# The end of an attention and two-layer mixture kernel: products in TensorE's gaps, another order of the merge, four banks for the last results

## The chip, the cores and the metric

The kernel runs on one core of a Trainium2 chip. A core has TensorE for matrix products (weights are loaded by its own instruction, which the profile shows as PEld), VectorE (DVE), ScalarE (ACT), GpSimd (POOL) and SyncE (SP), which here only starts transfers. Products end in PSUM, which has eight banks; VectorE and ScalarE read them from there. The metric is the device time of one launch, in microseconds (us), the median of several runs.

## The reference

Three layers follow one another. The first is windowed attention over 4 sequences of 576 tokens with 8 heads of 64. Its output is a table of 2304 tokens by 512. The second layer is gated: `sigmoid(x @ w_gate) * (x @ w_val) @ w_out` with an inner width of 1536. The third is a soft mixture of 8 experts with 4 slots each:

```python
logits = x @ phi                                  # 2304 x 32 slots
d = logits - logits.max(0, keepdims=True)         # softmax over the tokens, per slot
d = np.exp(d)
d /= d.sum(0, keepdims=True) + 1e-09
slot_input = (d.T @ x).reshape(E, S_per_e, D)     # 32 slots x 512
for e in range(E):
    h = np.maximum(slot_input[e] @ w1[e], 0.0)    # 4 x 1024
    slot_out[e] = h @ w2[e]                       # 4 x 512
c = logits - logits.max(1, keepdims=True)         # softmax over the slots, per token
c = np.exp(c)
c /= c.sum(1, keepdims=True) + 1e-09
return c @ slot_out                               # 2304 x 512
```

The softmax over the tokens runs over all 2304 tokens, so the expert products can start only when the last token block has been seen.

## The kernel before

The tokens are worked in five blocks: four of 512 and a short one of 256 (the last 64 tokens of each sequence). Attention, the gated layer (`l1`, `l2`) and the slot sums (`moe2`) go through the blocks, interleaved in the order of the program. A scheduler may move an instruction forward on its engine when its inputs and buffers allow; `tc.keep_in_program_order` takes that freedom from an instruction. Each engine then works its list strictly in order, TensorE too.

`moe2(n, last)` (L456) takes a block's second-layer output. It transposes it (tp), forms the logits (lt_ps), and keeps a running maximum mrun, sum lrun and slot sum acc per slot, in the manner of an online softmax: nm holds the new maximum and the factor that scales what was there; d is the exponential of the logits less the maximum, dt its transpose, and sp the block's share of the slot sum. Tokens are held in up to four groups of 32 rows, one for each 128 tokens, with maxima of their own. For the last block `merge` (L432) brings the four groups together: it transposes mrun (rows), takes the maximum over the groups, subtracts, takes the exponential (L448), and turns the four weights back into a column (wcol) and a 128 x 32 table i4w. With it, st_ps (L660) sums acc over the groups, and the result, st, is what the experts read.

The expert layer follows. h_ps (L670) is the product with w1 for all 8 experts, with four column groups at a time; after it come ht_ps, so_ps (L729, with w2, first for the left 256 columns of the output, dh = 0, then for the right, dh = 1), `scale` (by the reciprocal of the sums), `gather` (sr_ps: the sum over column groups, split into two parts), and `result` (L751): the product op of each token's weights ct with sr, for two token tiles at a time into one of the two PSUM banks of the pool ps_l1. ScalarE copies the first two tiles of a block to ob, VectorE the other two, and SP sends ob to memory: 512 KB for each of the four large blocks, and four transfers of 64 KB for the short one. The left half's results are put between the so_ps products of the right half. The weights of the experts come in 32 transfers of 1 MB as buffers come free (`load_e`).

At the very start of the kernel `keep_warm` (L110) lets TensorE multiply a table of zeros in bfloat16 while it waits for its first data.

## Time and profile before

| | us |
|---|---|
| median of 3 runs | 621.69 (621.18 to 622.74) |
| the profiled execution, its own time | 622.22 |
| its span, first to last instruction | 620.4 |
| TensorE busy (share of the span) | 593.7 (96%) |
| VectorE busy | 305.5 (49%) |
| ScalarE busy | 269.2 (43%) |
| GpSimd busy | 185.6 (30%) |

The span is what the trace covers; the time of the launch is 1.82 us longer. Busy shares are means over the whole span. The last 68 us, from the end of the second layer for the short block, are the stretch in which the change lies. The granted clock over the whole span is 0.977 of full speed. In a timeline's row the bracket at the end says how long the engine was idle before it and which instruction ended that; a row may join several instructions (x48).

### The profile page before, as it was taken

What the parts mean: (1) busy time and instruction counts of PE and PEld (TensorE: products, weight loads), DVE (VectorE), ACT (ScalarE), POOL (GpSimd) and SP (SyncE); (2) the same over time, 40 slices, a digit from 0 to 9 for tenths busy, and PEclk for the clock granted to TensorE, in tenths of its full rate; (3) what the DMA queues carried; (4) which work ended last, traced back from release to release, by engine and by line L of the source; (5) the groups of instructions that cost most, each with busy time, mean ns of one, the idle gap of its engine ahead of it and who ended that gap; (6) DMA issues with size and microseconds to landing.
All of it is one profiled execution on the core that took longest, in us unless ns stands there. A gap on an engine that the chain in (4) does not pass through costs nothing.

```text
span 620.4 us, 11601 instructions
## 1 busy us (share of the span) xinstructions
PE 593.7 (96%) x4849; PEld 454.5 (73%) x4849; DVE 305.5 (49%) x544; ACT 269.2 (43%) x456; POOL 185.6 (30%) x147
## 2 busy tenths in 40 slices
PE   7898999999999999999999999999999899988994
PEld 4667777777777776777788888888878789863452
DVE  5978565645344556574422232312455666662342
ACT  3798454353535454555322122312454485540122
POOL 1344435432134542461101010302534524431100
PEclk9899999999999999999999999999999999996996
DMA  8988759882244351669010011028313724787965
GB/s 348 375 312 277 257 171 396 300 310 67 69 179 163 123 187 46 226 214 364 17 69 28 41 68 69 0 78 327 138 69 148 280 81 173 299 342 300 423 236 199
DMA packets 24933, 120.46 MB, mean 194 GB/s; under 512 B 2480, under 2 KB 7344, under 8 KB 14768
## 3 DMA queue, kind: packets, MB, share of 16 engines
q1 hardware_dynamic: 24880, 119.71, 52.2%
q8 instruction: 38, 0.62, 0.4%
q14 instruction: 15, 0.12, 0.1%
HBM read 105.55 MB, written 14.16 MB: 193 GB/s over the span
## 4 chain that ended last, share of the span: by engine, by line
PE 79%; ACT 6%; POOL 5%; issue 5%; DVE 3%; DMA 2%; ACTq 0%; DVEq 0%; POOLq 0%; SPq 0%
PE l1ps L372 46%; PE acc L411 13%; POOL l2t L404 4%; PE xp L192 3%; PE h_ps L670 3%; PE so_ps L729 2%; PE s_ps L139 2%; ACT l2t L402 2%; PE tr L177 1%; PE tp L467 1%; ACT bd L180 1%; PE op L760 1%; PE lt_ps L475 1%; PE sp L513 1%; DMA qk<-qkv 1%
## 5 line engine op out<-in xcount | busy, mean ns | idle before, releaser
L372 PE MATMUL l1ps<-x_hi,whl 128*128 128x512 f32 x768 | 248.6, 397 | 0.0
L372 PEld LDWEIGHTS l1ps<-x_hi,whl 128*128 128x128 f32 x768 | 144.8, 189 | 31.7 <-issue 0.4
L411 PE MATMUL acc<-l2t 128*128 128x512 f32 x648 | 159.4, 397 | 1.6 <-POOL l2t L404 1.6
L372 PE MATMUL l1ps<-x_lo,whl 128*128 128x512 f32 x384 | 150.7, 392 | 0.0
L411 PEld LDWEIGHTS acc<-l2t 128*128 128x128 f32 x648 | 118.6, 188 | 27.8 <-POOL l2t L404 2.0
L404 POOL TENSOR_TENSOR l2t<-wos,l2t 128x512 fp32r<-128x512 f32 x54 | 72.1, 1338 | 124.3 <-ACT l2t L402 120.7
L384 DVE TENSOR_TENSOR g<-l1ps,g 128x512 f32<-128x512 f32 (+1 forms) x60 | 38.2, 637 | 135.0 <-PE l1ps L372 134.9
L407 DVE TENSOR_TENSOR l2t<-g,l2t 128x512 fp32r<-128x512 f32 (+1 forms) x60 | 66.0, 1100 | 53.5 <-ACT l2t L406 52.6
L372 PEld LDWEIGHTS l1ps<-x_lo,whl 128*128 128x128 f32 x384 | 72.6, 189 | 14.2
L382 ACT ACTIVATE g<-l1ps 128x512 f32<-128x512 f32 (+1 forms) x60 | 33.3, 555 | 105.7 <-PE l1ps L372 105.5
L339 POOL TENSOR_TENSOR whl<-wst,whl 128x512 fp32r<-128x512 f32 x28 | 38.4, 1372 | 131.0 <-ACT whl L338 131.0
L402 ACT CAST l2t<-wos 128x512 fp32r<-128x512 f32 x60 | 37.0, 620 | 80.2 <-PE acc L411 27.0
L326 POOL TENSOR_TENSOR fw<-fw 128x512 int32<-128x512 int32 x36 | 49.1, 1373 | 75.7 <-DVE fw L324 33.6
L338 ACT CAST whl<-wst 128x512 fp32r<-128x512 f32 x56 | 31.9, 618 | 36.5 <-PE l1ps L372 28.0
L339 DVE TENSOR_TENSOR whl<-wst,whl 128x512 fp32r<-128x512 f32 x28 | 36.4, 1302 | 14.5 <-ACT whl L338 14.5
L372 PE MATMUL l1ps<-x,whl 128*128 128x256 f32 x288 | 36.4, 286 | 0.8 <-ACT g L382 0.5
L372 PEld LDWEIGHTS l1ps<-x,whl 128*128 128x128 f32 x288 | 35.1, 192 | 1.5 <-ACT g L382 0.7
L406 ACT CAST l2t<-g 128x512 fp32r<-128x512 f32 (+1 forms) x60 | 34.4, 573 | 1.7 <-DVE g L384 1.6
L192 PEld LDWEIGHTS xp<-bd,v 128*64 128x64 f32 x608 | 20.2, 139 | 13.6 <-ACT bd L180 9.0
L192 PE MATMUL xp<-bd,v 128*64 128x64 f32 (+1 forms) x608 | 23.6, 228 | 5.4 <-ACT bd L180 3.6
L180 ACT COPY bd<-tr 64x512 f32<-64x512 f32 x40 | 23.1, 578 | 8.0 <-PE tr L177 7.7
L152 DVE TENSOR_REDUCE mx<-s_ps 128x4 f32<-128x256 f32 x40 | 15.5, 418 | 21.7 <-PE s_ps L139 21.7
(128 smaller groups left out, 505.2 us busy)
## 6 DMA issues: line engine op xcount, KB each, us to landing
ew<-w SPq DMA_DIRECT2D x32, 1024.0 KB, 7.0
st<-wd SPq DMA_DIRECT2D x18, 1024.0 KB, 7.6
wos<-wo SPq DMA_DIRECT2D x15, 1024.0 KB, 4.7
wst<-wg SPq DMA_DIRECT2D x14, 1024.0 KB, 4.8
v<-qkv SPq DMA_DIRECT2D x20, 512.0 KB, 7.4
wg<-fw SPq DMA_DIRECT2D x12, 512.0 KB, 8.2
qk<-qkv SPq DMA_DIRECT2D x10, 576.0 KB, 4.9
qk<-qkv SPq DMA_DIRECT2D x8, 528.0 KB, 3.7
```

The costliest lines, as they stand in the source:

```text
L192: nc.tensor.matmul(o, lhsT=v[:, t, i, r, :], rhs=b_[:, 2 * r + t, i, :, 0:nq], start=True, stop=True)
L326: nc.gpsimd.tensor_tensor(low.bitcast(I32), top.bitcast(I32), low.bitcast(I32), ALU.add)
L338: nc.scalar.copy(whl[:, 0, h], src[:, h])
L339: (nc.gpsimd if pool[h] else nc.vector).tensor_tensor(whl[:, 1, h], src[:, h], whl[:, 0, h].bitcast(F32), ALU.subtract)
L372: nc.tensor.matmul(pt[:, 0:nt], lhsT=whl[:, w_, a, dc, :], rhs=x_[n][:, dc, :], start=first, stop=(dc == HP_ORDER[-1] and w_ == 1),)
L382: nc.scalar.activation(g, pt[:, 0:nt], AF.Sigmoid)
L384: nc.vector.tensor_tensor(g, pt[:, 0:nt], g, ALU.mult)
L402: nc.scalar.copy(woh, wos[:, f % 4])
L404: eng.tensor_tensor(wol, wos[:, f % 4], woh.bitcast(F32), ALU.subtract)
L406: nc.scalar.copy(gh[:, 0:nt], g)
L407: nc.vector.tensor_tensor(gl[:, 0:nt], g, gh[:, 0:nt].bitcast(F32), ALU.subtract)
L411: nc.tensor.matmul(accs[j], lhsT=g_[:, c], rhs=w_, start=(f == 0 and g_ is gh and w_ is woh), stop=(f == NF - 1 and g_ is gl),)
```

## The change

- `keep_busy(count)` issues bfloat16 products of 512 columns on TensorE, from the mask table that lies in SBUF from the start, into a bank that nobody reads: 2 behind the last block's transposes, 4 behind its logits, 2 behind wcol, 2 behind st_ps, and 4 behind the last sr_ps. 14 in all.
- `merge` is split. In the last block d, its exponential and its transpose come first, then the merge's maximum, subtraction and exponential (`merge_rows`), and wcol and i4w (`merge_weights`) come behind sp. The update of acc is done in two halves of 256 columns in the last block. In the other blocks the transpose of d also comes ahead of its sum.
- `result` takes PSUM banks from ps_a as well as from ps_l1: for the left half the short block's, for the right half every second pair of pairs, so that four banks take turns. The left half's short block comes behind the last so_ps products.
- The right half's four transfers of the short block are issued by ScalarE, not by SP.
- Some instructions are kept in program order.

TensorE's list from the logits of the last block to the expert layer, before (x_5128 is the last block's second-layer output, t_5161 the tile that holds the merge's pieces and st):

```order
L475 MATMUL lt_ps<-xt,cst 32x128 x8
L438 MATMUL rows<-cst,mrun 1x128
L450 MATMUL wcol<-cst,t_5161 128x1
L508 MATMUL dt_ps<-cst,d 128x64
L513 MATMUL sp<-x_5128,dt 32x512 x2
L660 MATMUL st_ps<-t_5161,acc 128x32 x4
L691 MATMUL sums<-cst,lrun 1x128
L670 MATMUL h_ps_5202<-ew,t_5161 32x512 x4
```

The same stretch of TensorE's list now, from the last of the four products behind the logits to st_ps:

```order
L124 MATMUL busy<-msk 128x512
L516 MATMUL dt_ps<-cst,d 128x64
L451 MATMUL rows<-cst,mrun 1x128
L530 MATMUL sp<-x_5128,dt 32x512 x2
L466 MATMUL wcol<-cst,t_5175 128x1
L124 LDWEIGHTS msk
L124 MATMUL busy<-msk 128x512
L124 LDWEIGHTS msk
L124 MATMUL busy<-msk 128x512
L681 MATMUL st_ps<-t_5175,acc 128x32 x4
```

dt_ps stands ahead of rows and wcol, wcol stands behind sp, and two added products stand between wcol and st_ps.

ScalarE's list in the same stretch, before (nm is the running maximum's factor, t_5161 here the merge's exponential):

```order
L493 ACT_TABLE_LOAD
L493 ACTIVATE nm<-nm 64x1
L448 ACTIVATE t_5161<-t_5161 1x128
L499 ACTIVATE d<-d 64x128
L535 ACTIVATE c<-c 128x64
```

And now:

```order
L510 ACT_TABLE_LOAD
L510 ACTIVATE nm<-nm 64x1
L514 ACTIVATE d<-d 64x128
L461 ACTIVATE t_5175<-t_5175 1x128
L556 ACTIVATE c<-c 128x64
```

The exponentials of d and of the merge have changed places.

TensorE's list at the end of the right half, before (ct_5267 holds the short block's token weights):

```order
L729 MATMUL so_ps_5336<-ew,ht 32x256 x8
L760 MATMUL op<-sr,cts 128x256 x4
L760 MATMUL op<-sr,ct_5267 128x256 x2
L729 MATMUL so_ps_5336<-ew,ht 32x256 x16
L745 MATMUL sr_ps<-t_5161,cst 128x256
L760 MATMUL op<-sr,cts 128x256 x16
```

And now, up to the first of the four products behind sr_ps:

```order
L751 MATMUL so_ps_5348<-ew,ht 32x256 x8
L790 MATMUL op<-sr,cts 128x256 x4
L751 MATMUL so_ps_5348<-ew,ht 32x256 x16
L790 MATMUL op<-sr,ct_5279 128x256 x2
L769 MATMUL sr_ps<-t_5175,cst 128x256
L124 LDWEIGHTS msk
L124 MATMUL busy<-msk 128x512
```

The left half's short block has gone from ahead of the last 16 so_ps products to behind them.

```diff
--- before.py
+++ after.py
@@ -112,6 +112,19 @@
             nc.tensor.matmul(idle, lhsT=zero[:, 0:P], rhs=zero[:, 512:1024], start=True, stop=True)
 
     keep_warm(WARM)
+    busy = {}
+
+    kept = tc.keep_in_program_order
+
+    def keep_busy(count):
+        if "ps" not in busy:
+            busy["ps"] = ps_a.tile([P, 512], F32, tag="a", name="busy")
+        for _ in range(count):
+            kept(
+                nc.tensor.matmul(
+                    busy["ps"], lhsT=msk[:, M_ID:M_COLS], rhs=msk[:, 0:512], start=True, stop=True, skip_group_check=True
+                )
+            )
 
 
     x_hi, x_lo = {}, {}
@@ -429,7 +442,7 @@
     share = []
     first_pb = [True]
 
-    def merge():
+    def merge_rows():
         t1 = b8("l2", [P, 2048], F32, "t1")
         st, so = t1[:, 0:1152].rearrange("p (k x) -> p k x", k=ND), t1[:, 1152:1664]
         sc_ = t1[:, 1664:2048]
@@ -437,7 +450,7 @@
         rows = ps_m.tile([1, P], F32, tag="m", name="rows")
         nc.tensor.transpose(rows, mrun, ident)
         rm = sc_[0:1, 0:32]
-        nc.vector.tensor_reduce(rm, rows.rearrange("o (j s) -> o s j", j=4), AX.X, ALU.max)
+        kept(nc.vector.tensor_reduce(rm, rows.rearrange("o (j s) -> o s j", j=4), AX.X, ALU.max))
         re = sc_[0:1, 32:160].rearrange("o (j s) -> o j s", j=4)
         nc.vector.tensor_tensor(
             re,
@@ -446,12 +459,12 @@
             ALU.subtract,
         )
         nc.scalar.activation(re, re, AF.Exp)
+        return st, so, sc_, re, sc_[:, 160:192]
+
+    def merge_weights(re, i4w):
         wcol = ps_m.tile([P, 1], F32, tag="m", name="wcol")
         nc.tensor.matmul(wcol, lhsT=re.rearrange("o j s -> o (j s)"), rhs=ident[0:1, 0:1], start=True, stop=True)
-        i4w = sc_[:, 160:192]
         nc.vector.tensor_tensor(i4w, i4, wcol.to_broadcast([P, 32]), ALU.mult)
-        return st, so, sc_, re, i4w
-
 
     def moe2(n, last):
         xs = x2_sb.pop(n)
@@ -469,6 +482,8 @@
                 nc.vector.tensor_copy(xt[:, j], tp)
             else:
                 nc.scalar.copy(xt[:, j], tp)
+        if last:
+            keep_busy(2)
         lt_ps = ps_m.tile([P, P], F32, tag="m", name="lt_ps")
         for kc in range(ND):
             for j in range(ntt):
@@ -481,6 +496,8 @@
                 )
         lt = cpool.tile([P, P], F32, tag="lt", name="lt", bufs=2)
         nc.vector.tensor_copy(lt[0:np_], lt_ps[0:np_])
+        if last:
+            keep_busy(4)
         first = first_pb[0]
         first_pb[0] = False
         nm = sm.tile([P, 4], F32, tag="nm", name="nm")
@@ -492,11 +509,15 @@
             nc.vector.tensor_tensor(nm[0:np_, 1:2], mrun[0:np_], nm[0:np_, 0:1], ALU.subtract)
             nc.scalar.activation(nm[0:np_, 1:2], nm[0:np_, 1:2], AF.Exp)
             nc.vector.tensor_copy(mrun[0:np_], nm[0:np_, 0:1])
-        if last:
-            merged = merge()
         d = cpool.tile([P, P], F32, tag="d", name="d")
         nc.vector.tensor_scalar(d[0:np_], lt[0:np_], mrun[0:np_, 0:1], None, ALU.subtract)
         nc.scalar.activation(d[0:np_], d[0:np_], AF.Exp)
+        dt_ps = ps_m.tile([P, P], F32, tag="m", name="dt_ps")
+        nc.tensor.transpose(dt_ps[:, 0:np_], d[0:np_], ident[0:np_, 0:np_])
+        dt = cpool.tile([P, P], F32, tag="dt", name="dt")
+        nc.vector.tensor_copy(dt[:, 0:np_], dt_ps[:, 0:np_])
+        if last:
+            merged = merge_rows()
         if first:
             nc.vector.tensor_reduce(lrun, d, AX.X, ALU.add)
         else:
@@ -504,10 +525,6 @@
             nc.vector.scalar_tensor_tensor(
                 lrun[0:np_], lrun[0:np_], nm[0:np_, 1:2], nm[0:np_, 2:3], ALU.mult, ALU.add
             )
-        dt_ps = ps_m.tile([P, P], F32, tag="m", name="dt_ps")
-        nc.tensor.transpose(dt_ps[:, 0:np_], d[0:np_], ident[0:np_, 0:np_])
-        dt = cpool.tile([P, P], F32, tag="dt", name="dt")
-        nc.vector.tensor_copy(dt[:, 0:np_], dt_ps[:, 0:np_])
         sp = ps_m.tile([P, 512], F32, tag="m", name="sp")
         for j in range(ntt):
             nc.tensor.matmul(
@@ -516,9 +533,13 @@
         if first:
             nc.vector.tensor_copy(acc, sp)
         else:
-            nc.vector.scalar_tensor_tensor(
-                acc[0:np_], acc[0:np_], nm[0:np_, 1:2], sp[0:np_], ALU.mult, ALU.add
-            )
+            if last:
+                merge_weights(merged[3], merged[4])
+                keep_busy(2)
+            for c in (slice(0, 256), slice(256, 512)) if last else (slice(0, 512),):
+                nc.vector.scalar_tensor_tensor(
+                    acc[0:np_, c], acc[0:np_, c], nm[0:np_, 1:2], sp[0:np_, c], ALU.mult, ALU.add
+                )
         if last:
             return merged, lt
         shares(n, ntt, lt)
@@ -662,6 +683,7 @@
         st.rearrange("p k (e x) -> p k e x", x=36)[:, :, :, 0:4],
         st_ps.rearrange("p k (e a) -> p k e a", a=4),
     )
+    keep_busy(2)
     h_ps = [ps_a.tile([P, 512], F32, tag="a", name=f"h_ps{h}") for h in range(2)]
     reuse = ["qk", "qk", "v", "v", "xb", "xb", "ga", "gb", "gb", "gb"]
     for e in range(8):
@@ -726,13 +748,15 @@
     def expert(dh, e):
         for fc in range(8):
             c = fc % 4
-            nc.tensor.matmul(
+            ins = nc.tensor.matmul(
                 so_ps[dh][32 * c : 32 * c + 32],
                 lhsT=ht[fc // 4][:, c, 32 * e : 32 * e + 32],
                 rhs=ew[1, dh, e].rearrange("p a c -> p (a c)")[:, 256 * fc : 256 * fc + 256],
                 start=(e == 0 and fc < 4),
                 stop=(e == 7 and fc >= 4),
             )
+            if dh:
+                kept(ins)
 
     def scale(dh):
         so_, _ = half(dh)
@@ -742,22 +766,28 @@
     def gather(dh):
         so_, sr_ = half(dh)
         sr_ps = ps_m.tile([P, 256], F32, tag="m", name="sr_ps")
-        nc.tensor.matmul(sr_ps, lhsT=ones32, rhs=so_, start=True, stop=True)
+        kept(nc.tensor.matmul(sr_ps, lhsT=ones32, rhs=so_, start=True, stop=True))
         nc.scalar.copy(sr_, sr_ps)
         nc.vector.tensor_tensor(sr_[64:P], sr_ps[64:P], sr_[64:P].bitcast(F32), ALU.subtract)
 
     obs = {}
+    n_op = [0]
+    Z_ORDER = (0, 1, 2, 3, 4)
 
     def result(dh, z):
         _, sr_ = half(dh)
         n, ntt, ct = ct_sb[z]
-        if z % 2 == 0:
-            obs[dh] = b8(("x2", "ws", "ws")[z // 2], [P, 2, 4, 256], F32, "ob")
-        ob = obs[dh][:, z % 2]
+        k = Z_ORDER.index(z)
+        if k % 2 == 0:
+            obs[dh] = b8(("x2", "ws", "ws")[k // 2], [P, 2, 4, 256], F32, "ob")
+        ob = obs[dh][:, k % 2]
         for j in range(0, ntt, 2):
-            op = ps_l1.tile([P, 2, 256], F32, tag="l1", name="op")
+            more = k == 4 if dh == 0 else n_op[0] // 2 % 2
+            n_op[0] += dh
+            pool, tag = (ps_a, "a") if more else (ps_l1, "l1")
+            op = pool.tile([P, 2, 256], F32, tag=tag, name="op")
             for y in range(2):
-                nc.tensor.matmul(op[:, y], lhsT=ct[:, j + y], rhs=sr_, start=True, stop=True)
+                kept(nc.tensor.matmul(op[:, y], lhsT=ct[:, j + y], rhs=sr_, start=True, stop=True))
             if j == 0:
                 nc.scalar.copy(ob[:, j : j + 2], op)
             else:
@@ -767,7 +797,7 @@
             nc.sync.dma_start(out[576 * n : 576 * n + 512, d].rearrange("(a p) d -> p a d", p=P), ob)
         else:
             for b in range(4):
-                nc.sync.dma_start(
+                (nc.scalar if dh else nc.sync).dma_start(
                     out[576 * b + 512 : 576 * b + 576, d], ob[64 * (b % 2) : 64 * (b % 2) + 64, b // 2]
                 )
 
@@ -782,11 +812,14 @@
         expert(1, e)
         if e == GA:
             gather(0)
-        if GA < e <= GA + 5:
-            result(0, e - GA - 1)
+        if GA < e <= GA + 4:
+            result(0, Z_ORDER[e - GA - 1])
+    result(0, Z_ORDER[4])
     scale(1)
     gather(1)
-    for z in range(5):
+    busy["ps"] = ps_m.tile([P, 512], F32, tag="m", name="busy")
+    keep_busy(4)
+    for z in Z_ORDER:
         result(1, z)
 
 
```

## Rows read from the trace of the kernel before

**Rows 1.** Timeline of TensorE, last block to expert layer; columns: start, length (us), engine, line, ...
```profile
554.94 1.39 PE L475 MATMUL lt_ps<-xt,cst 128*32 128x128 f32 x16 [0.35 <-DVE xt L469]
557.66 0.27 PE L438 MATMUL rows<-cst,mrun 128*1 128x128 f32 x1 [1.33 <-DVE mrun L494]
558.95 0.58 PE L450 MATMUL wcol<-cst,t 1*128 1x1 f32 x2 [1.02 <-ACT t L448]
559.47 0.37 PE L508 MATMUL dt_ps<-cst,d 64*128 64x64 f32 x1
560.15 1.92 PE L513 MATMUL sp<-x,dt 128*32 128x512 f32 x4 [0.32 <-DVE dt L510]
562.91 1.92 PE L660 MATMUL st_ps<-t,acc 128*128 128x32 f32 x8 [0.84 <-DVE acc L519]
564.64 0.40 PE L691 MATMUL sums<-cst,lrun 128*1 128x128 f32 x1
565.28 6.78 PE L670 MATMUL h_ps<-ew,t 128*32 128x512 f32 x48 [0.24 <-DVE t L661]
...
576.08 5.36 PE L670 MATMUL h_ps<-ew,t 128*32 128x512 f32 x48
```

**Rows 2.** Stretches: PE, PEld, DVE, ACT, POOL busy (count); granted clock; DMA share; GB/s.
```profile
556.00:558.00 2.00, 0.59 (x6) 0.14 (x2) 1.32 (x7) 0.72 (x2) 0.00 (x0) 0.99 0.97 410
558.00:560.00 2.00, 0.88 (x3) 0.68 (x3) 0.95 (x5) 0.51 (x2) 0.00 (x0) 0.50 1.05 442
...
566.00:568.00 2.00, 2.00 (x16) 0.55 (x12) 0.56 (x3) 0.00 (x0) 0.00 (x0) 0.50 0.04 8
568.00:570.00 2.00, 2.00 (x24) 0.52 (x20) 0.00 (x0) 0.00 (x0) 0.00 (x0) 0.95 0.86 246
```

**Rows 3.** Timeline of TensorE, the last result.
```profile
603.47 0.51 PE L760 MATMUL op<-sr,ct 128*128 128x256 f32 x2 [0.44 <-ACT ob L762]
603.90 1.93 PE L729 MATMUL so_ps<-ew,ht 128*32 128x256 f32 x32
606.71 0.70 PE L745 MATMUL sr_ps<-t,cst 128*128 128x256 f32 x2 [0.87 <-ACT t L740]
608.33 0.73 PE L760 MATMUL op<-sr,cts 128*128 128x256 f32 x4 [0.93 <-DVE sr L747]
609.55 1.22 PE L760 MATMUL op<-sr,cts 128*128 128x256 f32 x4 [0.49 <-ACT ob L762]
```

**Rows 4.** Stretches of half a microsecond at the end, same columns as rows 2.
```profile
610.50:611.00 0.50, 0.28 (x2) 0.00 (x0) 0.18 (x1) 0.47 (x1) 0.00 (x0) 0.50 0.39 141
611.00:611.50 0.50, 0.47 (x2) 0.48 (x2) 0.50 (x1) 0.00 (x0) 0.00 (x0) 0.50 1.09 389
...
618.50:619.00 0.50, 0.00 (x0) 0.00 (x0) 0.00 (x0) 0.00 (x0) 0.00 (x0) 0.50 0.51 131
```

**Rows 5.** Timeline of VectorE, then of ScalarE: copies of the last result.
```profile
609.10 0.69 DVE L764 COPY ob<-op 128x512 f32<-128x512 f32 x1 [0.82 <-PE op L760]
...
614.89 0.59 ACT L762 COPY ob<-op 128x512 f32<-128x512 f32 x1 [0.93 <-PE op L760]
```

**Rows 6.** Timeline of SP's queue: the short block's transfers, first and second half.
```profile
604.62 3.22 SPq L770 DMA_DIRECT2D out<-ob  x4
...
615.50 2.40 SPq L770 DMA_DIRECT2D out<-ob  x4
```

**Rows 7.** Timeline of VectorE, then of ScalarE, beside rows 1.
```profile
557.55 0.28 DVE L498 TENSOR_SCALAR d<-lt,mrun 64x128 f32<-64x128 f32 x1
...
562.12 0.74 DVE L519 SCALAR_TENSOR_TENSOR acc<-acc,nm,sp 64x512 f32<-64x512 f32 x1 [1.91 <-PE sp L513]
...
558.59 0.31 ACT L448 ACTIVATE t<-t 1x128 f32<-1x128 f32 x1 [1.02 <-DVE t L442]
558.81 0.29 ACT L499 ACTIVATE d<-d 64x128 f32<-64x128 f32 x1
```

**Rows 8.** Timeline of TensorE near the start: bfloat16 products of 512 columns.
```profile
8.49 0.81 PE L112 MATMUL idle<-zero 128*128 128x512 bf16 x3
```

## The prediction

> **What bounds the kernel now.** I read the page first, then TensorE's order of time for the last 70 us, then the same stretch on VectorE and ScalarE, then the granted clock in short stretches, and last the output queue. The page says that TensorE is busy for 593.7 of 620.4 us, so most of the kernel is its work, and the change does not touch that work. What it touches is the end, where TensorE waits in two places.
>
> The first place lies between the last output product of the last token block and the first product of the expert layer, h_ps, at 565.28. There TensorE runs short products, each of which waits for another engine [rows 1]: 1.33 us before rows, 1.02 us before wcol (released by ScalarE), 0.84 us before st_ps. The clock falls there. It is 0.99 in 556 to 558, where TensorE is busy for 0.59 of 2.00 us, 0.50 in 558 to 560, still 0.50 in 566 to 568, and 0.95 in 568 to 570 [rows 2]. 0.50 is the lower of the two levels (1.2 of 2.4 GHz). So sp, st_ps and the first h_ps products run at half speed: 48 h_ps products take 6.78 us at the start and 5.36 us later [rows 1], a difference of 1.42 us.
>
> The second place is the last half of the result: after so_ps TensorE waits 0.87 and 0.93 us, and then 0.49 us for ScalarE to empty a bank [rows 3]; the clock is 0.50 again by 610.5 [rows 4], and the last copy of a result begins at 614.89 [rows 5]. Only then can the short block's four transfers go, which takes SP 2.40 us to 617.9 [rows 6].
>
> **The change part by part, up to h_ps.** *Exponential first.* ScalarE now does the exponential of d before that of the merge [rows 7]: d is subtracted at 557.55 to 557.83, yet its exponential ran at 558.81, behind the merge's at 558.59, which itself waited 1.02 us for VectorE. In the new order it starts at 557.88 and ends 0.29 later, at 558.17. dt_ps stood behind wcol and started at 559.47 [rows 1]; it can now start at 558.2, 1.25 us earlier. What is late next is the merge: its row maximum, subtraction (0.28 us each) and exponential (0.31 us, [rows 7]) come after the copy of dt and end near 559.9; that is about when sp ends, so wcol, now behind sp, waits little.
>
> *The products in the gaps.* 14 bfloat16 products of 512 columns are added: 2 ahead of lt_ps, 4 behind it, 2 ahead of st_ps, 2 behind it, 4 ahead of the last results. Three such products took 0.81 us at full clock, tails included [rows 8], so at most 0.27 us each; sp's four products of 512 columns took 1.92 us at half clock [rows 1], so at most 0.48 us each there. The first 2 fall into the 0.35 us wait before lt_ps, and lt_ps then waits for its second half anyway; I count 0 to 0.2, and take 0. The next 4 begin when lt_ps ends (556.33, 1.33 us ahead of rows [rows 1]) and end at 557.4, or at 558.25 at half clock; dt_ps is not ready before 558.2, so they cost nothing. The 2 ahead of st_ps run beside VectorE, which needs about 0.74 us for acc (now in two halves) [rows 7] and some 0.2 for the merge's weights; nothing, or 0.5 at half clock. The 2 behind st_ps and then sums stand ahead of h_ps: 0.54 + 0.2 against the 0.45 us that VectorE's copy of st takes anyway (st_ps ends at 564.83, h_ps starts at 565.28): +0.3.
>
> *What the clock gives.* In the new order TensorE's longest idle time in this stretch is the 0.8 to 1.0 us before dt_ps, and its busy time from 556 to 560 is about 2.9 us where [rows 2] has 1.47. I take it that the clock stays up. Then sp starts at 558.2 + 0.2 + 0.32 = 558.75 and takes 1.0; wcol ends at 560.3; products to 560.8; st_ps 1.0 (half of 1.92, and its second half waits for the second half of acc) to 561.8; products and sums to 562.5. h_ps starts at 562.5, not 565.28: 2.8 us. Its first 48 products give 1.42 more [rows 1]. Together **4.2 us**; bounds 0 (rival 1) and 4.6 (the last products free too).
>
> The Trainium skill's page "TensorE: Matmul & The Clock Gate", under "Why this matters for your kernels", speaks against this part: it names only idle gaps over a length more than twice the longest gap here as what brings the low clock. The trace disagrees: the clock fell with no gap over 1.33 us [rows 1, 2]. By the rule the products would give nothing, and the sum would be rival 1's.
>
> **The last results.** The result of the short block's first half moves behind the last so_ps products. Its 0.44 us wait for a bank and its own 0.43 us go from ahead of so_ps, which starts at 603.0 instead of 603.90 [rows 3]. ScalarE however still copies that result before it scales: so_ps ends at 604.9, the pair takes 0.51, the copy 0.59 [rows 3, 5], the scaling some 0.4 (about half of the 0.87 us that the two scalings took before); sr_ps starts near 606.35 instead of 606.71: 0.36 us. The 4 products behind it take 4 x 0.27 = 1.08 or less against a wait of 0.93 [rows 3]: 0 to 0.15. The results then go round four banks instead of two, and at full clock. Before, each waited for ScalarE's copy [rows 3]; now VectorE's 0.69 us per copy [rows 5] sets the pace, 0.72 per block. The first block's copy ends at 609.43 (was 609.79), the last full one at 611.6, the short block's near 611.9 (was 615.48).
>
> From there the transfers set the end. Four of 512 KB and four of 64 KB are 2.36 MB. Before, data began 1.0 us after the first copy's end (about 610.8) and stopped by 619.0 [rows 4], 1.4 us ahead of the span's end. Now the queue is never empty: at the 389 GB/s of a full half microsecond [rows 4] 2.36 MB take 6.06 us, from 610.44 to 616.5, and the span would end at 617.9. Two covers must hold. ScalarE's buffer for the short block waits for the transfers of the first half, which SP now issues from about 606.0 (the end of that copy) instead of 604.62 in up to 3.22 us [rows 6]; with 2.5 us behind the last issue, as at the end of the span, they land near 611.7, when ScalarE wants the buffer, so 0 to 1 us for that copy. And ScalarE issues its four in 2.4 to 3.2 us [rows 6], to 614.3 at the earliest and 616.1 at the latest; with the 2.5 us that lay behind the last issue before, 616.8 to 618.6. I take 617.9: the tail is **2.5 us** shorter, with bounds 0.45 (rival 2) and 3.0.
>
> The skill's page "DMA: Bandwidth & Descriptors", under "Rules for kernel authors", says that transfers from several engines share the same DMA engines, so that a second queue saves issue time alone. No row here has a second queue; by the rule the 617.9 stands and ScalarE's queue saves only SP's turn.
>
> **Sum.** The profiled execution took 622.22 us with a span of 620.4. 620.4 - 4.2 - 2.5 = 613.7, and 615.5 with the 1.8 us around it. The median shown is 621.69, 0.5 below the profiled one, so 615.0; I say **615.2**, because small waits are more often left out than counted twice. Its own range is 613.5 to 617. Elsewhere the order is nearly unchanged: in the earlier blocks one copy moves ahead of a small sum.
>
> **Rivals.**
> 1. *The clock falls all the same.* For it: at half speed TensorE was already busy for most of 560 to 568 and the clock came back only in 568 to 570 [rows 2]. Against it: the gaps are shorter and the added products are dense. Then dt_ps still starts at 558.2, sp ends at 560.7, wcol at 561.3, two products at 0.48 to 562.2, st_ps at 564.1, two products and sums at 565.4: h_ps starts where it did, and an earlier return of the clock gives 0 to 1.4. With a tail of 1.6 to 2.5 the time is 617.8 to 620.1, near 619.
> 2. *The transfers keep their pace.* For it: 2.36 MB in the 8.2 us from 610.8 to 619.0 is 288 GB/s, and single half microseconds with data are as low as 131 [rows 4]. Against it: those lows lie where the queue ran empty. Then the end is 610.44 + 8.2 + 1.4 = 620.0, the tail gives 0.45, and the time is 617.0.
> 3. *Slower: the added products are in the way.* They stand in TensorE's order, so what follows them waits, ready or not. At half clock 14 of them are 14 x 0.48 = 6.7 us. For it: the stretch is at half clock now. Against it: 6 of the 14 lie in waits that stay. If all were on the path, with 1.25 back from the exponential and 1.6 from the banks, the time is 621.69 + 3.9 = 625.6. It decides once more than 6 of them (2.9 us) are on the path.
> 4. *It does little*: the banks and the order take the place of other waits, and the clock falls as before: 620.5.
>
> **How the numbers follow.** Forecast 0.60, rival 1 0.18, rival 2 0.13, rival 3 0.04, rival 4 0.05. About 0.3%, 1.9 us, is what a measurement of this kernel tells from no change, so faster is under 619.8: the forecast, rival 2 and three quarters of rival 1, 0.86; same 0.09, with rival 4 and the rest of rival 1; slower 0.05, rival 3 and a little for what I don't see. The range 613.3 to 619.5 holds the forecast, rival 2 and most of rival 1.
>
> **What would show it.** dt_ps close to 558.2 and ahead of wcol shows the exponential. A granted clock near 1.00 through 558 to 568, sp and st_ps near 1.0 us and h_ps near 562.5 show the products; 0.50 there shows rival 1. In the tail, with everything 4.2 us earlier: no wait of a result for a bank, the last copy 3.5 us closer to so_ps, DMA at 350 GB/s or more without holes; holes show rival 2. Wrong outright would be an h_ps start later than 565.3, or a last transfer that begins after 613 in the new time.

## The result, and the profile after

The changed kernel took a median of 615.46 us (615.32 to 616.70 in 4 executions) against 622.22 us of the kernel before, timed beside it (621.18 to 623.96 in 4): a ratio of 0.9886, interval 0.9864 to 0.9907. It is faster, and 615.2 was forecast. The profiled execution took 615.44 us with a span of 613.7 us.

TensorE's timeline after, from the last block's transposes to the expert layer (start, length, engine, line, tiles, count, idle time before and what ended it), answers to [rows 1]:

```profile
554.94 1.38 PE L490 MATMUL lt_ps<-xt,cst 128*32 128x128 f32 x16
556.25 1.04 PE L124 MATMUL busy<-msk 128*128 128x512 bf16 x4
558.21 0.27 PE L516 MATMUL dt_ps<-cst,d 64*128 64x64 f32 x1 [0.93 <-ACT d L514]
558.41 0.27 PE L451 MATMUL rows<-cst,mrun 128*1 128x128 f32 x1
558.80 1.05 PE L530 MATMUL sp<-x,dt 128*32 128x512 f32 x4
559.78 0.38 PE L466 MATMUL wcol<-cst,t 1*128 1x1 f32 x2
560.09 0.60 PE L124 MATMUL busy<-msk 128*128 128x512 bf16 x2
560.53 1.07 PE L681 MATMUL st_ps<-t,acc 128*128 128x32 f32 x8
561.44 0.60 PE L124 MATMUL busy<-msk 128*128 128x512 bf16 x2
561.87 0.27 PE L713 MATMUL sums<-cst,lrun 128*1 128x128 f32 x1
562.08 5.36 PE L692 MATMUL h_ps<-ew,t 128*32 128x512 f32 x48
```

lt_ps starts at 554.94 as before, and h_ps 3.2 us earlier than the 565.28 of [rows 1]. The only wait of any length is the 0.93 us ahead of dt_ps, behind the four added products (busy). dt_ps now stands ahead of wcol; sp takes 1.05 us, st_ps 1.07 and the first 48 h_ps products 5.36, where [rows 1] has 1.92, 1.92 and 6.78. The granted clock of the same stretches (columns as in [rows 2]) is why:

```profile
556.00:558.00 2.00, 1.29 (x8) 0.36 (x5) 1.29 (x6) 0.86 (x3) 0.00 (x0) 1.00 1.02 430
558.00:560.00 2.00, 1.67 (x8) 0.58 (x8) 1.18 (x6) 0.47 (x2) 0.00 (x0) 1.00 1.00 422
566.00:568.00 2.00, 2.00 (x22) 0.67 (x18) 0.16 (x1) 0.00 (x0) 1.33 (x2) 1.00 1.00 418
568.00:570.00 2.00, 2.00 (x24) 0.65 (x20) 0.00 (x0) 0.00 (x0) 0.73 (x1) 1.00 0.99 422
```

It is 1.00 throughout, where it was 0.50 from 558 to 568 before. TensorE was busy for 1.29 and 1.67 of the first two stretches of 2 us, not 0.59 and 0.88.

ScalarE's timeline shows the new order, for [rows 7]: the exponential of d is ahead of the merge's (t).

```profile
557.85 0.31 ACT L514 ACTIVATE d<-d 64x128 f32<-64x128 f32 x1 [0.29 <-DVE d L513]
559.36 0.31 ACT L461 ACTIVATE t<-t 1x128 f32<-1x128 f32 x1 [1.20 <-DVE t L455]
603.84 3.04 ACT L792 COPY ob<-op 128x512 f32<-128x512 f32 x5 [1.10 <-PE op L790]
606.90 4.06 ACTq L800 DMA_DIRECT2D out<-ob  x4
```

Its last two rows answer to [rows 5, 6]: five copies run one after the other with no wait for a buffer, and then the four small transfers are issued, over 4.06 us. TensorE's timeline of the last result, for [rows 3]:

```profile
598.32 1.93 PE L751 MATMUL so_ps<-ew,ht 128*32 128x256 f32 x32
600.18 0.51 PE L790 MATMUL op<-sr,ct 128*128 128x256 f32 x2
601.63 0.70 PE L769 MATMUL sr_ps<-t,cst 128*128 128x256 f32 x2 [0.94 <-ACT t L764]
602.17 1.03 PE L124 MATMUL busy<-msk 128*128 128x512 bf16 x4
603.25 2.50 PE L790 MATMUL op<-sr,cts 128*128 128x256 f32 x16
605.70 0.51 PE L790 MATMUL op<-sr,ct 128*128 128x256 f32 x2
```

The results run through with no wait for a bank. VectorE's copies of them, for [rows 5], follow each other as closely:

```profile
604.03 2.58 DVE L794 COPY ob<-op 128x512 f32<-128x512 f32 x4 [0.83 <-PE op L790]
```

The output in stretches of 1 us, for [rows 4]; the last two columns are DMA share and GB/s:

```profile
605.00:606.00 1.00, 1.00 (x8) 0.85 (x7) 1.00 (x3) 0.94 (x2) 0.00 (x0) 1.00 0.28 99
606.00:607.00 1.00, 0.20 (x2) 0.00 (x0) 0.60 (x2) 0.72 (x2) 0.00 (x0) 1.00 1.09 388
...
609.00:610.00 1.00, 0.00 (x0) 0.00 (x0) 0.00 (x0) 0.00 (x0) 0.00 (x0) 0.50 1.10 377
...
611.00:612.00 1.00, 0.00 (x0) 0.00 (x0) 0.00 (x0) 0.00 (x0) 0.00 (x0) 0.50 0.99 342
612.00:613.00 1.00, 0.00 (x0) 0.00 (x0) 0.00 (x0) 0.00 (x0) 0.00 (x0) 0.50 0.08 25
```

The transfers are dense from 606 to 612 and the holes of [rows 4] are gone. In finer stretches the first bytes move at 605.7 and the last at 612.2, so the span ends 1.5 us after the data.

Stage lengths of every profile, in us, from the starts of the last block's first transpose (tp), h_ps, ht_ps and the second sr_ps, and the end of the span:

| kernel | tp to h_ps | h_ps to ht_ps | ht_ps to sr_ps | sr_ps to end | sum |
|---|---|---|---|---|---|
| before | 11.78 | 16.11 | 25.32 | 13.69 | 66.90 |
| changed | 8.59 | 14.67 | 24.88 | 12.07 | 60.21 |
| e1_no_fill | 9.00 | 17.31 | 24.87 | 12.03 | 63.21 |
| e2_fill_only | 9.88 | 14.68 | 24.94 | 12.57 | 62.07 |
| e3_exp_only | 8.98 | 17.33 | 25.31 | 13.47 | 65.09 |
| e4_tail_only | 11.47 | 17.30 | 24.88 | 12.01 | 65.66 |
| e5_sp_queue | 8.59 | 14.68 | 24.87 | 12.47 | 60.61 |
| e6_two_banks | 8.59 | 14.68 | 24.88 | 12.63 | 60.78 |
| e7_fill_x2 | 9.38 | 15.94 | 24.87 | 12.58 | 62.77 |
| e8_fill_4_4 | 8.59 | 16.03 | 24.88 | 12.05 | 61.55 |
| e9c_again (the changed kernel) | 8.59 | 14.68 | 24.87 | 12.05 | 60.19 |
| e9_dve_scale | 8.59 | 14.68 | 24.10 | 12.02 | 59.39 |
| e10_two_issues | 8.59 | 14.68 | 24.10 | 11.81 | 59.18 |
| e11_fill_l2 | 8.59 | 14.68 | 24.10 | 11.81 | 59.18 |

The table is the better measure of each edit. tp itself starts anywhere from 552.4 to 557.6, since the clock also falls in earlier stages, in some executions and not in others. That before and after both have it at 553.5 is luck. A stage in which the clock stays up repeats within 0.05 us from profile to profile where the instructions are the same. A stage with a fall in it does not: e4_tail_only has the instructions of the kernel before up to ht_ps, and its first two stages take 28.77 us where that kernel's take 27.89, since the fall came at another moment.

### The profile page after: what moved, and what is told of

Its sections match the earlier page's. It is cut to its first block, busy times and chain, and to the rows that moved or that the text cites. A ratio compares the mean times of both kernels' runs of the same rounds, so it can differ in the third digit from the quotient of the medians.

```text
span 613.7 us, 11630 instructions
## 1 busy us (share of the span) xinstructions
PE 590.3 (96%) x4863; PEld 452.6 (74%) x4863; DVE 305.7 (50%) x545; ACT 269.1 (44%) x456; POOL 185.1 (30%) x147
## 4 chain that ended last, share of the span: by engine, by line
PE 74%; POOL 6%; issue 5%; ACT 4%; DMA 2%; DVE 1%; ACTq 0%; DVEq 0%; POOLq 0%; SPq 0%
PE l1ps L385 44%; PE acc L424 14%; POOL l2t L417 4%; PE so_ps L751 2%; PE h_ps L692 2%; PE xp L205 2%; ACT l2t L415 2%; PE tp L480 1%; PE s_ps L152 1%; PE lt_ps L490 1%; PE op L790 1%; PE tr L190 1%; PE sp L530 1%; DMA qk<-qkv 1%; DMA wos<-wo 1%
```

## The experiments

The first four take the change apart, the next four change one size, and the last four look for more. "Before" is always the kernel before, timed in the same set on the same chip.

### e1_no_fill: the changed kernel without the 14 products

```diff
-        for _ in range(count):
+        for _ in range(0):
```

> The changed kernel without its 14 added products; all else of the change stays. Theory A (the products hold the clock where TensorE waits): the granted clock falls to 0.50 near 558 again and stays low into the h_ps products; sp and st_ps take 1.9 us each instead of 1.05 and 1.07, h_ps starts near 563.7 instead of 562.08 and its first products are at half clock; in the last results the clock falls too, but the transfers hide most of it. Time 618.8 us (617.8 to 620), some 3.3 above the changed kernel. Rival B (the clock is not the products' doing, the new order and the banks give the gain): clock near 1.00 through 558 to 566, h_ps at 562 or earlier, time 615.0 to 615.8. Rival C (the products are in the way): faster than the changed kernel, 614 or less.

Median 619.90 us (617.51 to 621.48 in 10); ratio 0.9941, interval 0.9915 to 0.9967. The stretches of 1 us in its profile show the clock fall and come back:

```profile
561.00:562.00 1.00, 0.76 (x6) 0.29 (x2) 0.50 (x3) 0.27 (x1) 0.00 (x0) 1.00 1.05 442
562.00:563.00 1.00, 0.87 (x6) 0.88 (x7) 0.46 (x2) 0.00 (x0) 0.00 (x0) 0.80 0.97 410
...
569.00:570.00 1.00, 1.00 (x12) 0.32 (x8) 0.00 (x0) 0.00 (x0) 0.00 (x0) 0.78 0.97 401
```

Without the products the clock goes to 0.50 in 562 to 563 (7.5 us behind tp), and the stage from h_ps to ht_ps takes 17.31 us, 2.64 more. h_ps starts only 0.41 us later. So ten of the products are worth 3.0 us (63.21 against 60.21), nearly all as the rate of h_ps and hardly any as its start. The other four, behind the second sr_ps, do nothing here: that last stage is 12.03 us without them and 12.07 with them, and the first result starts 1.62 us behind sr_ps in both. One thing came out otherwise than expected: the fall was to come near 558, with sp and st_ps at 1.9 us each, but it came behind sp, and they took 1.05 and 1.51.

### e2_fill_only: the kernel before with the 14 products

The products stand in the old order, and those of the last results are kept in the written order, which the added ones need; that also moves the short block's first result by one expert.

```diff
+        if last:
+            keep_busy(2)
         lt_ps = ps_m.tile([P, P], F32, tag="m", name="lt_ps")
...
+        if last:
+            keep_busy(4)
...
+            if last:
+                keep_busy(2)
...
+    keep_busy(2)
     h_ps = [ps_a.tile(...)]
...
+    keep_busy(4)
     for z in range(5):
```

> The kernel before with the 14 added products alone, in its old order (merge ahead of the exponential, two banks, SP's queue; the short block's first half lands one expert later in TensorE's list). Theory A in its narrow form (the products alone hold the clock): clock 1.00 through 558 to 568, h_ps starts near 563.4, 4 us less than before in all, 618. Theory A with the order as a second condition (the old order leaves rows, wcol and dt_ps as short products between waits from 557.3 to 560.1, which the products do not fill): the clock falls in this stretch after all, a little later than before, h_ps starts near 565 and the front gives 0 to 1; the last results at full clock with two banks give 1: 620 to 621. Rival C (in the way): 622.5 or more.

Median 621.16 us (619.07 to 623.87 in 10); ratio 0.9972, interval 0.9944 to 1.0000. In its profile the clock is 1.00 throughout this stretch, as two of its rows show, although idle time ahead of rows and wcol is there again (0.36 and 1.02 us):

```profile
562.00:564.00 2.00, 0.64 (x4) 0.43 (x3) 1.06 (x6) 0.51 (x2) 0.00 (x0) 1.00 0.99 418
564.00:566.00 2.00, 1.63 (x7) 0.30 (x7) 0.87 (x3) 0.00 (x0) 0.00 (x0) 1.00 1.03 434
```

By stages this kernel gains 4.83 us (66.90 to 62.07), 3.33 of them up to ht_ps; by the medians only some 1.5 (before: 622.65). Part of the difference lies ahead of the stretch: this execution had three earlier falls, and tp started at 557.63. Eight of its ten executions have a lower mean clock (0.981 to 0.987) than the profiled one (0.989), so the profile shows one of the better ones. How often the clock falls in the old order with the products, only more profiles would tell; one can't say that they suffice there. The last stage is 1.12 us shorter too, with the old banks and queue: the clock is 1.00 through the last results, where the kernel before has 0.50 by 610.5 [rows 4] (more in e6_two_banks).

### e3_exp_only: the new order up to h_ps, without the products, with the old end

```diff
-        for _ in range(count):
+        for _ in range(0):
...
-    for z in Z_ORDER:
+    for z in range(5):
         result(1, z)
```

(The rest of the end is the kernel before's as well: two banks, SP's queue. The new order includes acc in two halves.)

> The new order of exponential and merge (with acc in two halves) alone: no added products, two banks, SP's queue, the old order of the last results. Theory A: dt_ps starts at 558.2, 1.25 us earlier, the clock falls all the same, so h_ps starts 1.3 to 1.6 us earlier than before and its first products stay slow; the tail is as before: 620.5 (620 to 621). Rival B (the order gives the front its whole gain): clock stays up, h_ps at 562, 617.5.

Median 621.29 us (619.30 to 623.40 in 10); ratio 0.9968, interval 0.9939 to 0.9996. Two products of its TensorE timeline, and the stretches around the second:

```profile
557.74 0.27 PE L516 MATMUL dt_ps<-cst,d 64*128 64x64 f32 x1 [1.89 <-ACT d L514]
560.05 1.50 PE L681 MATMUL st_ps<-t,acc 128*128 128x32 f32 x8 [0.36 <-DVE t L467]
```

```profile
560.00:561.00 1.00, 0.95 (x7) 0.95 (x7) 0.38 (x1) 0.00 (x0) 0.00 (x0) 0.77 1.04 442
561.00:562.00 1.00, 0.76 (x6) 0.42 (x5) 0.35 (x2) 0.00 (x0) 0.00 (x0) 0.50 0.97 410
```

h_ps starts 8.98 us behind tp, 2.80 earlier than before; 1.3 to 1.6 was expected. Of the 2.80, 1.24 us is the earlier dt_ps (4.73 us behind tp instead of 5.97), and 1.29 is that sp and st_ps take 1.05 and 1.50 us instead of 1.92 each, because the clock falls only at 560.5, 3.0 us later behind tp than in the kernel before. Whether the order puts the fall off, or this execution merely had it late, is not shown. With the fall the next stage takes 17.33 us, 1.22 more than before.

Up to ht_ps the order alone is thus worth 1.58 us (26.31 against 27.89). The products bring 3.05 more on top of it (23.26), and 3.33 on top of the old order in the profile of e2_fill_only (24.56). With a fall in the stage such sums are good to about 1 us: against the 28.77 of e4_tail_only the order is worth 2.46, and between the two profiles without a fall (24.56 and 23.26) 1.30.

### e4_tail_only: the old order up to h_ps, the new end without its four products

```diff
+            more = k == 4 if dh == 0 else n_op[0] // 2 % 2
+            n_op[0] += dh
+            pool, tag = (ps_a, "a") if more else (ps_l1, "l1")
...
-                nc.sync.dma_start(
+                (nc.scalar if dh else nc.sync).dma_start(
...
+    result(0, Z_ORDER[4])
```

> The new end of the kernel alone (four banks, the short block's first half behind the last so_ps products, its last transfers on ScalarE's queue), no added products, the front as before. Theory A: the front is as before; the clock falls near 609 so the results go at 1.33 us per block instead of 1.47, the last copy ends 1 us earlier, the transfers run nearly without holes: 1.5 to 1.9 us less than before, 620.3. Rival D (the transfers keep their pace of 288 GB/s): 0.5 less than before, 621.5.

Median 620.31 us (619.21 to 625.72 in 10); ratio 0.9964, interval 0.9936 to 0.9992. The two last stages are 24.88 and 12.01 us, 0.44 and 1.68 less than before: together as much as the changed kernel's tail gains, without the products. The clock was expected to fall near 609, among the last results; it stayed at 1.00 until 613.9, past the last copy. At the end of its profile the transfers go at 383 GB/s:

```profile
613.00:614.00 1.00, 0.00 (x0) 0.00 (x0) 0.00 (x0) 0.00 (x0) 0.00 (x0) 0.96 1.08 383
```

So the rival by which they keep 288 GB/s is out: the slow pace before came from holes between copies.

### e5_sp_queue: the short block's last transfers on SP's queue

```diff
-                (nc.scalar if dh else nc.sync).dma_start(
+                nc.sync.dma_start(
```

> The changed kernel with the short block's last four transfers issued by SP again, behind its four large ones. Theory (the bytes set the end): SP is free 3.0 us after its first issue, its four small issues take 2.4 more, and the data of the large blocks are still under way then; from the start of the last sr_ps to the end of the span 12.1 us as in the changed kernel, within 0.5. Rival (SP's turn set the end, ScalarE's queue is worth something): 13 us or more. Time 615.0 to 617.

Median 616.47 us (615.02 to 617.13 in 4); ratio 0.9899, interval 0.9878 to 0.9919. SP's queue in its profile:

```profile
604.99 3.00 SPq L797 DMA_DIRECT2D out<-ob  x4
608.08 3.64 SPq L800 DMA_DIRECT2D out<-ob  x4
```

SP issues the large ones until 608.0 and only then the small ones, to 611.7; the end comes 0.40 us later than in the changed kernel, within the 0.5 expected. From 606 to 611 data moves at 382 to 388 GB/s here and at 359 to 388 in the changed kernel, so the second queue saves some issue time and adds no rate. The Trainium skill's page "DMA: Bandwidth & Descriptors" states this rule under "Rules for kernel authors", and the trace agrees. The medians can't tell 0.4 us.

### e6_two_banks: the last results over two banks

```diff
-            more = k == 4 if dh == 0 else n_op[0] // 2 % 2
+            more = False
```

> The changed kernel with all results in the two banks of ps_l1. Theory (at full clock the copies set the pace, with four banks 0.72 us per block, with two some 1.2): last copy 1.9 us later, but the transfers hide part: 12.6 us from the last sr_ps to the end instead of 12.07. The left half's short block waits for a bank too, 0 to 0.1. Rival (the banks are what the tail gained, all of it): 13.5. Rival (the copies do not matter at all): 12.1.

Median 616.00 us (615.02 to 617.24 in 4); ratio 0.9892, interval 0.9867 to 0.9918. The wait for a bank is back, in its TensorE timeline:

```profile
605.01 0.80 PE L790 MATMUL op<-sr,cts 128*128 128x256 f32 x4 [0.48 <-ACT ob L792]
```

```profile
605.00:606.00 1.00, 0.80 (x4) 0.59 (x4) 0.40 (x2) 0.45 (x1) 0.00 (x0) 1.00 0.25 65
```

The last stage is 12.63 us, 0.56 longer, as expected. Taken away alone, four banks cost 0.56 of the tail's 2.06 us and the second queue 0.40. These two don't simply add: with two banks the queue makes no difference (12.63 with ScalarE's, 12.57 with SP's in e2_fill_only).

The earlier sr_ps is 0.44, and the remaining 1.06 us (13.69 to 12.63) goes with the clock: the same four products behind the same wait take 0.80 us here and 1.22 in [rows 3]. The clock fell among the last results in the kernel before and in e3_exp_only, which have two banks and no products behind sr_ps, and in no other profile. So four banks (e1_no_fill, e4_tail_only) or the four products with two banks (here and in e2_fill_only) went with a clock that stays up; each of the two is two profiles, and all four have the kept order as well.

### e7_fill_x2: twice as many products

```diff
-        for _ in range(count):
+        for _ in range(2 * count):
```

> The changed kernel with 28 added products instead of 14. Theory (a product costs what its wait does not cover, 0.216 us each): two more ahead of lt_ps cost 0.4, the four more behind it nothing (they end before dt_ps is ready), two more ahead of st_ps 0.4, two more behind it 0.4, four more ahead of the last results 0.8: h_ps starts 9.8 us after the last block's first transpose instead of 8.59, the first last result 2.4 after sr_ps instead of 1.62; 2.1 us more in all, 617.6. Rival (all 14 on the path at 0.27): 3.8 more. Rival (the products cost nothing): no more than 0.5.

Median 619.33 us (617.20 to 620.04 in 5); ratio 0.9943, interval 0.9923 to 0.9963. Its TensorE timeline ahead of dt_ps, and a place in the next stage:

```profile
556.71 1.90 PE L124 MATMUL busy<-msk 128*128 128x512 bf16 x8
558.68 0.27 PE L516 MATMUL dt_ps<-cst,d 64*128 64x64 f32 x1
...
568.50 0.27 PE L713 MATMUL sums<-cst,lrun 128*1 128x128 f32 x1
568.70 1.90 PE L692 MATMUL h_ps<-ew,t 128*32 128x512 f32 x10
570.65 0.35 PE L721 MATMUL rcol<-cst,t 1*128 1x1 f32 x2
```

The eight products fill the wait ahead of dt_ps and no wait is left there; h_ps starts 0.79 us later, not 1.2: the wait ahead of dt_ps takes up 0.3 us of what the products ahead of lt_ps cost, and sums, 0.2 us, no longer stands ahead of h_ps. The first last result comes 2.08 us behind sr_ps, 0.46 later. The other 1.27 us is a side effect that was not forecast: sums moved in among the h_ps products, and ten of these, up to rcol, take 1.90 us, where 48 in 5.36 make 1.12; the weights of two of the ten are loaded singly there, where four go together elsewhere. All in all 2.56 us are lost (2.1 expected), 1.25 of them at the products themselves: a product costs what the wait at its place does not cover. So added products can be in the way, as rival 3 had it. In the changed kernel they are not: with half as many h_ps starts earlier than with none (e1_no_fill).

### e8_fill_4_4: only the four products behind lt_ps, and the four at the end

```diff
-            keep_busy(2)
+            keep_busy(0)
```

(At all three places.)

> The changed kernel with 8 of its 14 added products: the four behind the logits and the four ahead of the last results; the pairs ahead of lt_ps and on both sides of st_ps are gone. Theory (the four in the long wait are what keeps the clock, the pairs are a safety that costs 0.3): clock up in all or most executions, h_ps starts 8.3 to 8.6 us after the first transpose, 615.0 to 616.5 us. Rival (the pairs are needed: wcol and st_ps are short products among waits): clock falls at the start of the h_ps products in many executions, 616.5 to 619 us, spread like that of the kernel without any added product.

Median 616.88 us (614.47 to 621.65 in 7); ratio 0.9912, interval 0.9883 to 0.9940. In its profile the clock falls again, at the end of st_ps:

```profile
561.00:562.00 1.00, 1.00 (x9) 0.86 (x9) 0.23 (x1) 0.00 (x0) 0.00 (x0) 0.90 1.00 426
562.00:563.00 1.00, 0.76 (x5) 0.20 (x8) 0.85 (x3) 0.00 (x0) 0.00 (x0) 0.50 1.07 451
```

h_ps starts at 8.59 us all the same, so the three pairs cost nothing at the start; the next stage is 1.36 us longer. So the four alone did not keep the clock up in this execution; the median lies with the rival (616.5 to 619) rather than with the 615.0 to 616.5 expected. By the medians it can't be told from the changed kernel, though its executions spread further; how often it needs the pairs stays open.

### e9c_again, e9_dve_scale, e10_two_issues, e11_fill_l2: further

These four ran in one set: the changed kernel again; with the second half's scaling whole on VectorE rather than half on ScalarE, behind its copy; with that, and the last transfers of both halves in two issues of twice the size and the first large one cut in two; and with that, six added products ahead of the wait in an earlier stage (the second layer of the last full block, near 491), where the clock falls as well.

```diff
+        if dh:
+            nc.vector.tensor_scalar(so_, so_ps[dh], rc[:, 0:1], None, ALU.mult)
+            return
...
-            for b in range(4):
+            rest = out.rearrange("(a h r) d -> h r a d", a=2, h=2)
+            for h in range(2):
                 (nc.scalar if dh else nc.sync).dma_start(
-                    out[576 * b + 512 : 576 * b + 576, d], ob[64 * (b % 2) : 64 * (b % 2) + 64, b // 2]
+                    rest[h, 512:576, :, d], ob[64 * h : 64 * h + 64, 0:2]
...
+            if n == 3 and f == 10:
+                for _ in range(6):
+                    kept(nc.tensor.matmul(fill, lhsT=msk[:, M_ID:M_COLS], rhs=msk[:, 0:512], ...))
```

> The changed kernel once more, as the base of this set: 615.3 to 616.7 us as before; 60.2 us from the last block's first transpose to the end of the span, 12.07 from the last sr_ps.

> The changed kernel with the scaling of the right half on VectorE alone, so that sr_ps no longer waits for ScalarE, which copies the left half's short block first (0.94 us of wait before sr_ps). Theory (the transfers run without a hole from the first copy on, so an earlier first copy moves the end by as much): from the last so_ps product to sr_ps some 0.75 us less, 59.4 us from the first transpose to the end, 0.8 us faster than the changed kernel. Rival (the last transfers wait for something else: the buffers that the left half's transfers still read, or ScalarE's own four issues of 4 us): 0 to 0.3 faster.

> The kernel before it, with the short block sent in two transfers of 128 KB instead of four of 64 KB, and the right half's first large block sent in two halves, the first one as soon as ScalarE has copied it. Theory: data begin 0.3 us earlier and the issues are done sooner, 59.1 us from the first transpose to the end, 1.1 us faster than the changed kernel. Rival (the bytes and the last landing decide alone): as the kernel before it, within 0.15.

> The kernel before it, with six more bfloat16 products in another wait: TensorE stands 1.55 us for GpSimd in the second layer of the last large block, near 488 us, and in several of the profiles the clock falls behind it for 3.4 to 3.9 us. Theory (the same cause as at the end): the clock stays up there in all executions, the last block starts 0 to 1.8 us earlier, median 1 us below the kernel before it and the spread smaller; 613.5 us. Rival (that fall has another cause): no difference, the clock falls there as often.

| kernel | median us (lowest to highest, 6 each) | ratio to before | interval |
|---|---|---|---|
| e9c_again | 616.37 (614.42 to 618.67) | 0.9911 | 0.9885 to 0.9937 |
| e9_dve_scale | 615.82 (614.09 to 618.12) | 0.9898 | 0.9869 to 0.9926 |
| e10_two_issues | 614.61 (613.43 to 617.77) | 0.9887 | 0.9860 to 0.9913 |
| e11_fill_l2 | 615.99 (612.56 to 617.89) | 0.9898 | 0.9868 to 0.9929 |

The wait ahead of the second sr_ps, in e9_dve_scale, is 0.17 us where the changed kernel has 0.94:

```profile
604.28 0.70 PE L772 MATMUL sr_ps<-t,cst 128*128 128x256 f32 x2 [0.17 <-DVE t L764]
```

Its stages sum to 59.39 us, 0.80 less than e9c_again, as expected. e10_two_issues takes another 0.21 off (0.3 was expected). It issues its last transfers in 1.94 us instead of 4.06, in ScalarE's queue:

```profile
607.67 1.94 ACTq L808 DMA_DIRECT2D out<-ob  x2
```

So 2.1 us less of issuing gave 0.21 us at most: the data, not ScalarE's turn, sets nearly all of the end. e10_two_issues and e11_fill_l2, which has the same end, are the best by stages, 1.01 us ahead of the changed kernel. The median of e10_two_issues is the lowest of the set; but the intervals overlap, and the times alone do not show it faster than the changed kernel.

e11_fill_l2 fills the wait that it aims at. TensorE there in e10_two_issues, in e9_dve_scale, and then in e11_fill_l2:

```profile
489.73 7.46 PE L424 MATMUL acc<-l2t 128*128 128x512 f32 x23 [1.54 <-POOL l2t L417]
```

```profile
493.20 5.88 PE L424 MATMUL acc<-l2t 128*128 128x512 f32 x23 [1.54 <-POOL l2t L417]
```

```profile
491.50 1.24 PE L425 MATMUL fill<-msk 128*128 128x512 bf16 x5
493.22 5.88 PE L433 MATMUL acc<-l2t 128*128 128x512 f32 x23 [0.24 <-POOL l2t L417]
```

The 23 products take 5.88 us, where e10_two_issues needs 7.46, as the clock stays at 1.00. This does not show that the six products did it: behind the same wait, and without them, the clock stayed up in e9_dve_scale too. Of the 13 profiles without the six, nine have the fall there and four do not. The lowest time of all, 612.56 us, is this kernel's, but the median is no better, and the 613.5 expected was missed: in its profiled execution the clock fell near 21 to 27 and 62 to 66 us. What these six products are worth over many executions stays open.

## Why the prediction was right

**The order up to h_ps: right, 0.4 us too small.** The forecast had dt_ps at 558.2, sp at 558.75, the end of wcol at 560.3, of st_ps at 561.8, and h_ps at 562.5. Measured were 558.21, 558.80, 560.16, 561.60 and 562.08. The difference comes at the end of the chain: I added whole durations, but a duration holds the tail of a pipelined product, beside which the next has begun. The two products behind st_ps have a length of 0.60 us, and sums starts 0.43 after them. The start gained 3.19 us where 2.8 was forecast, and the rate of the next stage 1.44 where 1.42 was: 4.63 against 4.2.

**What gives it: two things, the products more than the order.** The forecast put it all down to the clock staying up with both; it did not say how each would do alone. Of the 4.63 us the order alone gives 1.58 in the profile of e3_exp_only (1.3 to 2.5 by others): it brings h_ps forward by 2.80 and loses 1.22 again to the lower clock behind. The products give the other 3.05. Without them the stage from h_ps is 2.64 us longer (e1_no_fill), more than the 1.42 forecast from [rows 1]. That is no contradiction: the fall came later there than in the kernel before, and so more of it lay over h_ps.

**Rival 1, the clock falls all the same: wrong for this kernel.** The clock was 1.00 in all four stretches above, and the next stage is 14.67 or 14.68 us in all eight profiles with just these ten products; the clock fell in all four without any (the kernel before, e1_no_fill, e3_exp_only, e4_tail_only), one execution each. The rival was not far off, though: e8_fill_4_4, with four of the ten, lost 1.36 us to a fall. It also had the price in the wrong place: with a fall and the new order h_ps was to start where it did before, but in e1_no_fill it started 2.78 us earlier behind tp, and the loss lay in the stage behind.

The row on idle gaps of the Trainium skill's page "TensorE: Matmul & The Clock Gate", under "Why this matters for your kernels", names only gaps longer than any here as what brings the low clock, and by it the products would have given nothing. e3_exp_only disagrees with it as [rows 2] did, with a fall where the longest wait is 1.89 us, ahead of dt_ps.

**The tail: mechanism right, 0.44 us too large.** sr_ps came 0.44 us earlier (0.36 forecast), and from sr_ps to the end of the first VectorE copy (0.69 us as in [rows 5], from 604.03) it took 3.09 us (3.08 in the forecast). The copies kept pace, no buffer was waited for, and the last copy ended 606.88, 3.96 us earlier than before apart from the start's gain (53.39 behind tp against 61.98, less 4.63; 3.58 forecast). The transfers then set the end, as forecast. Data began 1.0 us behind that first copy, as forecast, and the span ended 1.5 us behind the data (1.4). The term that was mis-sized is the data itself: it took 6.5 us (605.7 to 612.2), not 6.06. The forecast gave all 2.36 MB the 389 GB/s of a full half microsecond; the mean was 363, with 377 to 342 in the last full microseconds and less at either edge. That is the 0.44 us; the 0.1 at the end and the 0.08 of sr_ps cancel.

That the results would run at full clock was forecast in passing. The tail rests on it as the start does: 1.06 of the 2.06 us go with the clock (e6_two_banks).

**ScalarE's issues: outside their bounds, without effect on the end to speak of.** They took 4.06 us, not 2.4 to 3.2. The last was out at 610.96, 2.7 us ahead of the end, close to the 2.5 us that lay behind the last issue before; so they were almost level with the data, and e10_two_issues, with 2.1 us less of them, gained 0.21.

**The four products behind the second sr_ps: idle.** They were put at 0 to 0.15 us of cost; in the new end they cost nothing and bring nothing (e1_no_fill, e4_tail_only).

**The sum.** 4.63 and 2.06 make 6.69 us, where 4.2 and 2.5 made 6.7: two errors of 0.4 us cancelled. What lay ahead of tp cancelled too, by chance, in the two profiled executions; the median of the repeat, 616.37 us, shows how far it can differ.

## What to carry to other kernels

Where TensorE waits between short products, add up two things: the wait itself, and what a lower clock costs the long products behind it. Here a new order of a few short instructions gave some 1.6 us by itself, and ten small products in the waits 3.0 on top of it, nearly all as the rate of the long products behind. Such products cost only what the wait at their place does not cover, unless they push another instruction to a worse place (e7_fill_x2), so they are counted against each wait, not added freely. Where a clock falls in some executions and not in others, one profile that stays up does not show that the products did it (e11_fill_l2).

At a tail of copies and transfers, look first for holes in the data; when they are closed, what is left is bytes by rate. Here a clock that stayed up through the results was worth about 1.1 us, and issue queues and banks mattered by tenths of a microsecond.

## What was unexpected of the hardware

- The clock falls also far from the change, in some executions and not in others. In the profile of the changed kernel it does so in the second layer of the last full block, where TensorE was busy for a whole microsecond at 0.50:

```profile
490.00:491.00 1.00, 1.00 (x3) 0.75 (x3) 0.39 (x1) 0.00 (x0) 0.00 (x0) 0.50 0.98 418
```

  Behind a wait of about 1.55 us there, the same in each, nine profiles have the fall and four do not. Executions of one kernel differ by some 4 us, as e9c_again's 614.42 to 618.67; the mean clock of its fastest is 0.995 and of its slowest 0.987.
- Also its moment varies: 4.5 us behind tp in the kernel before, 6.6 in e4_tail_only, which has the same order there, and 7.5 in e1_no_fill and e3_exp_only.
- Four transfers of 64 KB took ScalarE 4.06 us to issue, and SP 3.64 us in e5_sp_queue, against 2.40 us in [rows 6]: about 1.0 us each instead of 0.6. The DMA share was 1.08 and 1.09 meanwhile, and 0.81 in the case of [rows 6]; that this is the cause is not shown.
